# Attention beside a spectral filter on one core: the output projection as scaled fp16 parts on four column quarters, in four pieces a unit

## The chip, the cores and the metric

One Trainium2 chip; the kernel runs on one of its cores. The metric is device time in microseconds of one execution, as the median of the runs; lower is better. The parts that matter here: TensorE (PE, matrix products, with its weight loads shown as PEld), ScalarE (ACT, the exponentials), VectorE (DVE), GpSimd (POOL, which here mostly issues transfers) and SyncE (SP, which issues transfers).

## The reference

Two independent results are concatenated. A is attention with 16 query heads that share one key and one value head, over 2048 positions of 448 features (28 for each head); B is a 2-D spectral filter of a 2048 x 448 array.

```python
q = (x @ wq).reshape(B, S, H, Dh).transpose(0, 2, 1, 3)   # S=2048, H=16, Dh=28
k = x @ wk
v = x @ wv
scores = einsum("bhqd,bkd->bhqk", q, k) * Dh ** -0.5
p = softmax(scores)
o = einsum("bhqk,bkd->bhqd", p, v)
a = o.transpose(0, 2, 1, 3).reshape(B, S, H * Dh) @ wo

X = rfft2(x2)                                              # 2048 x 225
b = irfft2(X * (w_r + 1j * w_i))
return concatenate([a, b], axis=-1)
```

All inputs and outputs are float32.

## The kernel before

**Start.** The kernel projects queries, keys and values, transforms the first part of B's columns, and prepares a bound on each query's scores, so that the exponentials can run without a pass for the maxima. A planner (class `Plan`) orders this part. It is not touched.

**Main loop.** The 16 heads are four groups `g` of four; the 2048 queries are four chunks `c` of 512. The loop goes over 16 pairs (c, g), and in each over 16 blocks `kc` of 128 keys: 256 steps. A step is

- two score tiles (`scores`, line 1156): for each, eight matmuls with a stationary of 128 rows x 32 columns in fp16 and 512 moving columns, four of them side by side on the four 32-column quarters of the array. Three pairs of PSUM banks (0 to 5) take turns for them;
- two exponentials on ACT (line 1159), 128 x 1024 each, from PSUM into SBUF. Up to nine of these results may be waiting (`PAIRS`);
- one value product (`values`, line 1176): four fp32 matmuls on the four quarters, recorded as eight, into bank 6 or 7, which hold the running sum of the group.

When a group's 16 steps are over, DVE copies the sum out (`group_out`, line 1050), the denominators go through DRAM to be spread over the partitions (lines 1055 to 1063, all issued by POOL), and `group_norm` (lines 1072 to 1075) multiplies by the reciprocals and splits the result into a high part `oh` and a low part `ol`, both of type fp32r. Four spare rows of each 32-row block take copies of low parts by transfers (lines 1080 to 1085), so that fewer products are needed.

**Filler.** The bank of 6 and 7 that the current group does not use is the place for other PE work, handed out as units by queues in `work`:

- "l": what is left of B's first transform: 6 units `late_features` (line 171) and 8 units `late_points` (line 953). When the last of them has been evicted, `spectrum` starts B's long middle part on DVE, ended by a transfer through DRAM (`store`, line 901);
- "z": B's last transform, 16 units `z_unit` (line 997) and 16 units `y_unit` (line 1019), which follow that middle part;
- "w": the output projection of A, `w_unit` (line 1110): for one chunk and 128 queries, eleven fp32r matmuls of 128 x 128 by 448 columns (line 1094): high part by high weights, high by low, low by high, for four groups, where the first group lacks one of them. Twelve units for the first three chunks, available when a chunk's last group has been normalised. The fourth chunk is projected in the tail, in 48 such matmuls.

**Order.** The program order of the loop is fixed at build time by a small clock model (`clk`, `free`, `after`): it knows a nominal duration for each piece of PE, ACT and DVE work and runs the events of DVE in the order of their due times. `back` adds to `owed` at each step, `EARLY[0]` = 0.3 us until the last "l" unit is evicted, `EARLY[1]` = 0.13 until B's last transform opens, and from then on what is left divided by the steps up to step 244. A unit is placed when `owed` is positive and `filler` gives a bank (steps 1 to 13 of 16, and the bank free). `switch` adds 0.13 us to the model's PE clock whenever work on quarters and work on the whole array follow each other.

**Weights.** `wo_load` brings the seven blocks of `wo` (issued by POOL, line 756), `wo_split` makes `woh` and `wol` of them on DVE (lines 759, 761), the first four early in the loop.

**Tail.** After the loop: the last group's normalisation (lines 1247 to 1261, on ACT, DVE and POOL), beside it 36 of the 48 matmuls of the last chunk, then the last 12; ACT evicts (`last_out`, line 1105), and four transfers bring the result out.

Of the kernel before, what the change touches and what calls it, by code (L numbers as in the profile page):

```python
# [26 lines left out]
NG = 4  # L27
# [8 lines left out]
EARLY = 0.3, 0.13  # L36
# [63 lines left out]
def kernel(ctx: ExitStack, tc: tile.TileContext, t: dict):  # L100
# [623 lines left out]
    clk = {"pe": 1.9, "dve": 2.2, "act": 2.6, "mode": "s"}  # L724
# [23 lines left out]
    woh = ap.tile([128, 7, D], F32R, name="woh", bufs=1)  # L748
    wol = ap.tile([128, NG, D], F32R, name="wol", bufs=1)
# [8 lines left out]
    def wo_split(g):  # L758
        V.tensor_copy(woh[:, g], wo[g])
        if g < NG:  # L760
            TT(wol[:, g], wo[g], woh[:, g].bitcast(F32), op=ALU.subtract)
# [157 lines left out]
    work = {"l": deque(), "z": deque(), "w": deque()}  # L919
# [12 lines left out]
    def late_features(q, p):  # L932
# [10 lines left out]
        return "v", 0.86, go  # L943
# [3 lines left out]
    def late_points(q, p):  # L947
# [21 lines left out]
        return "v", 0.76, go  # L969
# [19 lines left out]
    def z_unit(q, e):  # L989
# [17 lines left out]
        return "v", 0.87, go  # L1007
# [3 lines left out]
    def y_unit(q, v):  # L1011
# [27 lines left out]
        return "v", 0.87, go  # L1039
# [7 lines left out]
    def group_out(c, g):  # L1047
        o = osb[c, g] = qraw[:, g, c * CW:c * CW + CW]
        b = acc(4 * c + g)
        V.tensor_copy(o, bank[b])  # L1050
# [15 lines left out]
    def group_norm(c, g):  # L1066
        if g == 0:
            assert c or bsl.get(5) or bsl.get(6)
            oh[c] = op.tile([128, NG, CW], F32R, name="oh")
            ol[c] = op.tile([128, NG, CW], F32R, name="ol")  # L1070
# [4 lines left out]
        TT(ol[c][:, g], o, h.bitcast(F32), op=ALU.subtract)  # L1075
        normed[c] += 1
        if c < NC - 1:
            if g == 0:
                lows[c] = dp.tile([128, CW], F32, name="lows", bufs=2)
                nc.sync.dma_start(lows[c], ol[c][:, 0].bitcast(F32))  # L1080
            rows = lows[c].rearrange("(i m r) n -> r i m n", i=4, r=4)
            if g == NG - 1:
                for r in range(4):
                    nc.sync.dma_start(oh[c][DH + r::32].bitcast(F32), rows[r, :, :4])
                    nc.sync.dma_start(ol[c][DH + r::32, 1:].bitcast(F32), rows[r, :, 4:7])
                after(clk["dve"] + 7.0, 0.0, work["w"].extend, [w_unit(c, k) for k in range(4)])

    def wo_mm(p, c, k, gs):
        s = slice(k * 128, k * 128 + 128)
        for g in gs:  # L1090
            spare = c < NC - 1
            for n, (x, w, m) in enumerate(((oh, woh, g), (oh, wol, g), (ol, woh, g + 3 * spare))):
                if n < 2 or g or not spare:
                    mm(p, x[c][:, g, s], w[:, m], start=(g == 0 and n == 0), stop=(g == NG - 1 and n == 2))  # L1094

    def wo_out(p, c, k):
        y = fp.tile([128, D], F32, name="ya", tag="al")
        V.tensor_copy(y, p)  # L1098
# [3 lines left out]
    def last_out(p, k):  # L1102
        r0 = (NC - 1) * CW + k * 128
        y = pp.tile([128, D], F32, name="yb", tag="p")
        nc.scalar.activation(y, p, AF.Copy)  # L1105
        (nc.scalar if k == 3 else nc.sync).dma_start(t["oa"][r0:r0 + 128], y)

    def w_unit(c, k):
        def go(b):
            wo_mm(bank[b][:, :D], c, k, range(NG))  # L1110
            after(clk["pe"] + 0.9, 0.65, out, b)
# [4 lines left out]
        return "s", 2.22, go  # L1116

    def switch(mode):
        if clk["mode"] != mode:
            clk["pe"] += 0.13  # L1120
            clk["mode"] = mode
# [6 lines left out]
    def filler(step):  # L1128

        b = 13 - acc(min(step, 255) // 16)  # L1130
        return b if step % 16 < 14 and step % 16 and free[b] <= clk["pe"] and any(work.values()) else None
# [256 lines left out]
```

## Time and profile before

| | |
|---|---|
| runs before | 599.91, 599.15, 600.58 us; median 599.91 |
| the profiled execution | 600.41 us, of which the profile's span is 598.3 |
| matmuls of the loop and the tail in this profile | scores x4096, values x2048, output projection x180 |
| busy, share of the span: DVE, POOL | 57%, 15% |
| DMA | 62.39 MB, mean 104 GB/s |

How to read it: a PE record's duration overlaps those of its neighbours, since matmuls are pipelined and four run side by side, so busy sums and means are larger than the time the array is held. The chain of waits gives each piece only the time up to the next piece, and its pieces can be added. A step that waits for nothing shows there as 0.86 us of scores (x16) and 0.86 us of values (x8). A stretch table gives the busy time of each engine between two points of the span, and the number of its instructions in parentheses.

### The profile page before, as it was taken

How to read it: one execution, taken by the hardware profiler on the slowest of the kernel's cores; microseconds unless marked ns; L12 is line 12 of the kernel's file. 1: busy time of each engine (PE TensorE's matmuls, PEld its weight loads, DVE VectorE, ACT ScalarE, POOL GpSimd, SP SyncE). 2: the span in 40 equal slices, each digit the busy share in tenths (PEclk: the TensorE clock that was granted, in tenths of full speed). 3: DMA queues.
4: the chain of work that ended last, by engine and by line, in shares of the span. 5: the costliest groups of instructions: out<-in, count | busy, mean ns of one | idle time of the engine just before them, and what ended most of it. 6: DMA issues, size and time to landing. Idle time of an engine off the chain costs nothing.

```text
span 598.3 us, 18675 instructions
## 1 busy us (share of the span) xinstructions
PE 589.9 (99%) x8017; PEld 297.6 (50%) x8017; DVE 338.9 (57%) x679; ACT 512.4 (86%) x580; POOL 91.2 (15%) x168
## 2 busy tenths in 40 slices
PE   9999899999999999999999999999999999999997
PEld 7877454544444444444444444454445545444446
DVE  5995715332389988889887876122443532234214
ACT  4644799999999999989898989888888886888992
POOL 1021100104210112120102012220201202020100
PEclk9999899999999999999999999999999999999999
DMA  8774712234712023331011146522333323211101
GB/s 291 245 251 121 189 50 79 64 119 128 279 60 66 19 78 105 119 94 55 27 55 41 35 163 207 152 82 71 102 104 108 128 75 131 70 41 51 38 18 61
DMA packets 37493, 62.39 MB, mean 104 GB/s; under 512 B 6405, under 2 KB 27621, under 8 KB 37401
## 3 DMA queue, kind: packets, MB, share of 16 engines
q1 hardware_dynamic: 29792, 39.99, 20.7%
q0 software_dynamic: 7472, 20.96, 11.5%
q8 instruction: 63, 1.03, 0.7%
q10 hardware_dynamic: 144, 0.23, 0.1%
q14 instruction: 22, 0.17, 0.1%
HBM read 39.94 MB, written 20.50 MB: 101 GB/s over the span
## 4 chain that ended last, share of the span: by engine, by line
PE 90%; DMA 5%; DVE 1%; ACT 1%; issue 1%; SPq 0%; POOL 0%; ACTq 0%; POOLq 0%; DVEq 0%
PE banks L1156 37%; PE banks L1176 35%; PE banks L1094 6%; PE banks L337 6%; PE banks L1019 2%; PE banks L997 2%; PE banks L171 2%; DMA t<-X 1%; DMA raw<-xw 1%; DMA sd<-qraw 1%; PE banks L953 1%; DVE X L825 1%; DMA rs<-sd 1%; DMA qa<-qd 1%; ACT yb L1105 0%
## 5 line engine op out<-in xcount | busy, mean ns | idle before, releaser
L1159 ACT ACTIVATE p<-banks 128x1024 f32<-128x1024 f32 x512 | 476.3, 1148 | 45.3 <-PE banks L1156 41.6
L1156 PE MATMUL banks<-qa,ka 128*32 128x512 f16 x4096 | 278.7, 381 | 2.2 <-DMA qa<-qd 2.2
L1176 PE MATMUL banks<-p,vs 128*32 128x512 f32 x2048 | 265.8, 592 | 0.0
L1156 PEld LDWEIGHTS <-ka 128*32 128x32 f16 x4096 | 120.9, 96 | 196.1 <-issue 149.9
L1176 PEld LDWEIGHTS banks<-p,vs 128*32 128x32 f32 x2048 | 65.6, 110 | 47.6 <-issue 1.2
L1055 POOL DMA_DIRECT2D sd<-qraw x15 | 9.2, 610 | 203.5 <-DVE qraw L1050 203.5
L1050 DVE COPY qraw<-banks 128x512 f32<-128x512 f32 x15 | 10.4, 691 | 46.6 <-PE banks L1176 46.6
L1063 POOL DMA_DIRECT2D R<-rd x60 | 30.5, 515 | 34.0 <-DMA rd<-rs 34.0
L825 DVE SCALAR_TENSOR_TENSOR X<-w,X 128x226 f32<-128x226 f32 (+2 forms) x72 | 34.0, 472 | 2.2
L1098 DVE COPY ya<-banks 128x448 f32<-128x448 f32 x12 | 7.5, 625 | 40.1 <-PE banks L1094 40.1
L1026 DVE COPY w<-banks 128x256 f32<-128x256 f32 x16 | 6.8, 425 | 41.2 <-PE banks L1019 41.2
L1003 DVE COPY z<-banks 113x512 f32<-113x512 f32 (+1 forms) x16 | 11.1, 691 | 25.7 <-PE banks L997 25.7
L1094 PE MATMUL banks<-woh,oh 128*128 128x448 f32 x64 | 24.6, 385 | 0.5 <-DVE z L1003 0.5
L337 PE MATMUL banks<-xh,wqh 128*128 128x512 f32 x64 | 24.0, 405 | 0.1
L1094 PE MATMUL banks<-wol,oh 128*128 128x448 f32 x64 | 23.2, 362 | 0.0
L337 PE MATMUL banks<-xh,wql 128*128 128x512 f32 x64 | 23.0, 390 | 0.0
L341 ACT ACTIVATE qraw<-banks 128x512 f32<-128x512 f32 x16 | 9.3, 594 | 14.9 <-PE banks L337 14.9
L1094 PE MATMUL banks<-woh,ol 128*128 128x448 f32 x52 | 18.8, 362 | 0.0
L1061 POOL DMA_DIRECT2D rd<-rs x15 | 8.2, 548 | 66.2 <-DVE rs L1060 54.8
L818 DVE SCALAR_TENSOR_TENSOR w<-X 128x113 f32<-128x113 f32 (+2 forms) x56 | 17.7, 355 | 0.1
L1094 PEld LDWEIGHTS banks<-woh,oh 128*128 128x128 f32 x64 | 12.0, 188 | 10.9 <-issue 4.2
L997 PEld LDWEIGHTS banks<-fi,c 128*32 128x32 f32 (+2 forms) x512 | 14.4, 107 | 6.1 <-issue 4.0
(127 smaller groups left out, 514.5 us busy)
## 6 DMA issues: line engine op xcount, KB each, us to landing
qa<-qd SPq DMA_DIRECT2D x64, 128.0 KB
ob<-yo SPq DMA_DIRECT2D x16, 256.0 KB
t<-bs SPq DMA_DIRECT2D x16, 226.0 KB
X<-t POOLq DMA_DIRECT2D x8, 452.0 KB, 6.5
wf<-w POOLq DMA_DIRECT2D x8, 452.0 KB, 3.7
c<-t POOLq DMA_DIRECT2D x8, 452.0 KB, 4.3
R<-rd POOLq DMA_DIRECT2D x60, 56.0 KB, 2.1
raw<-xa SPq DMA_DIRECT2D x6, 512.0 KB
```

Of the source, the lines that this page charges most:

```text
L171: mm(pa[r0:r0 + 32, e, 113 * k:113 * k + 113], f[:113, 2 * r + k, 2 * p + e, h], cs1[:113, 2 * r + k], start=True, stop=True)
L337: mm(pq[c, g], w[:, j, gs], x[:, j], start=(j == 0 and n == 0), stop=(j == 3 and n == 1))
L818: STT(out, y, sy, x, op0=ALU.mult, op1=ALU.add if c > 0 else ALU.subtract)
L825: todo(226 * n, lambda d=d, q=q: STT(both(d), t[0].rearrange("p r n f -> p r (n f)"), q, both(a), op0=ALU.mult, op1=ALU.add))
L997: mm(pz[r, j], fb["c2", q % 2][:, e, j, r], fb["fi", q % 2][:, j], start=True, stop=True)
L1003: V.tensor_copy(fb["z", q % 2, e][:w], view(bank[b], 4, 128)[:w].rearrange("p j (r n) -> p r j n", r=2))
L1019: mm(py[m:m + 32, k], cs3[:w, kind, m:m + 32], fb["z", q % 2, e][:w, r].rearrange("p j n -> p (j n)"), start=True, stop=True)
L1063: nc.gpsimd.dma_start(R[32 * i:32 * i + DH], rd[i:i + 1].to_broadcast([DH, CW]))
L1094: mm(p, x[c][:, g, s], w[:, m], start=(g == 0 and n == 0), stop=(g == NG - 1 and n == 2))
L1156: mm(bank[b + h][r], ka[:, k:k + 32], qa[c, g][:, 2 * p + h], start=True, stop=True)
L1159: nc.scalar.activation(pt[i], banks[:, b:b + 2], AF.Exp, scale=SCALE / UP / UP)
L1176: mm(bank[b][32 * i:32 * i + 32], vs[:, kc], pt[2 * st + i // 2][:, i % 2], start=(kc == 0), stop=(kc == 15))
```

## The change

Four things.

1. **Number format and shape.** `oh`, `ol`, `woh`, `wol` become fp16. The group's sums are multiplied by `scale_v` when they leave PSUM and the weights by `scale_w`, and the projected result by `back_w`. Each matmul of 128 x 128 by 448 becomes four of 128 x 32 by 448, on the four column quarters; the count of products is the same.
2. **Scales.** New function `largest`: two transfers bring four blocks of `wo`, a small one the mask; `go` takes the largest magnitudes of `vs` and of those blocks on DVE, writes them to DRAM and reads them back spread over all partitions; `fix` makes the scales of them. The weight loads move from 5.0 to 24.0 on the model's clock. The mask's load in the tail goes away.
3. **Pieces.** A `w_unit` is now one group's two or three products; it queues the next as "more", which takes precedence over all other filler, keeps the same bank, and is placed without regard to `owed` from step 13 of a group on. Other units start in steps 1 to 12.
4. **Model and pace.** `switch` goes; a piece counts 0.19 us a product; `EARLY[0]` is 0.22 in place of 0.3, and the total for the late pace counts 2.09 for a unit in place of 2.48.

The diff, without three further removals of the mode from a `return`, one further `switch("v")` and most of the unchanged lines:

```diff
@@ -33,7 +33,8 @@
-EARLY = 0.3, 0.13
+EARLY = 0.22, 0.13
+PEAK = 16384.0
@@ -721,7 +722,7 @@
-    clk = {"pe": 1.9, "dve": 2.2, "act": 2.6, "mode": "s"}
+    clk = {"pe": 1.9, "dve": 2.2, "act": 2.6}
@@ -745,8 +746,10 @@
     def wide(n):
...
-    woh = ap.tile([128, 7, D], F32R, name="woh", bufs=1)
-    wol = ap.tile([128, NG, D], F32R, name="wol", bufs=1)
+    woh = ap.tile([128, 7, D], F16, name="woh", bufs=1)
+    wol = ap.tile([128, NG, D], F16, name="wol", bufs=1)
+    scales = ap.tile([128, 5], F32, name="scales", bufs=1)
+    real, scale_v, scale_w, back_w = (scales[:, n:n + 1] for n in range(4))
@@ -756,9 +759,40 @@
     def wo_split(g):
-        V.tensor_copy(woh[:, g], wo[g])
+        V.tensor_scalar(woh[:, g], wo[g], scale_w, None, op0=ALU.mult)
...
-            TT(wol[:, g], wo[g], woh[:, g].bitcast(F32), op=ALU.subtract)
+            STT(wol[:, g], wo[g], scale_w, woh[:, g], op0=ALU.mult, op1=ALU.subtract)
+    def largest():
+        x = [scratch()[:, :2 * D].rearrange("p (g n) -> p g n", g=2) for _ in range(2)]
+        m = ap.tile([128, 4], F32, name="m", bufs=1)
+        for k in range(2):
+            nc.gpsimd.dma_start(x[k], t["wo"][:, 2 * k:2 * k + 2])
+        nc.gpsimd.dma_start(real, t["mask"])
+        def go():
+            V.tensor_reduce(m[:, 0:1], vs[:, :, :DH], axis=AX.XY, op=ALU.max, apply_absolute_value=True)
+            for k in range(2):
+                V.tensor_reduce(m[:, k + 1:k + 2], x[k], axis=AX.XY, op=ALU.max, apply_absolute_value=True)
+            TT(m[:, 1:2], m[:, 1:2], m[:, 2:3], op=ALU.max)
+            md = dp.tile([128, 2], F32, name="md")
+            nc.gpsimd.dma_start(md, m[:, :2])
+            w = scratch()[:, :256].rearrange("p (a b) -> p a b", b=2)
+            nc.gpsimd.dma_start(w, md.rearrange("(o a) b -> o a b", o=1).to_broadcast([128, 128, 2]))
+            after(clk["dve"] + 7.0, 1.0, fix, w)
+        def fix(w):
+            V.tensor_reduce(m[:, :2], w.rearrange("p a b -> p b a"), axis=AX.X, op=ALU.max)
+            V.tensor_scalar(m[:, :2], m[:, :2], 1e-30, None, op0=ALU.max)
+            V.tensor_scalar(m[:, 0:1], m[:, 0:1], 1.0 / UP, None, op0=ALU.mult)
+            V.tensor_scalar(m[:, 2:4], m[:, :2], 1.0 / PEAK, None, op0=ALU.mult)
+            TT(back_w, m[:, 2:3], m[:, 3:4], op=ALU.mult)
+            V.reciprocal(m[:, 2:4], m[:, 2:4])
+            V.tensor_copy(scale_w, m[:, 3:4])
+            V.tensor_scalar(scale_v, real, -1.0, 1.0, op0=ALU.mult, op1=ALU.add)
+            TT(real, real, m[:, 2:3], op=ALU.mult)
+            TT(scale_v, scale_v, real, op=ALU.add)
+        after(clk["dve"] + 4.0, 1.6, go)
@@ -916,7 +950,7 @@
-    work = {"l": deque(), "z": deque(), "w": deque()}
+    work = {"more": deque(), "l": deque(), "z": deque(), "w": deque()}
@@ -940,7 +974,7 @@
-        return "v", 0.86, go
+        return 0.86, go
@@ -1047,7 +1081,7 @@
     def group_out(c, g):
...
-        V.tensor_copy(o, bank[b])
+        V.tensor_scalar(o, bank[b], scale_v, None, op0=ALU.mult)
@@ -1065,24 +1099,23 @@
     def group_norm(c, g):
...
-            assert c or bsl.get(5) or bsl.get(6)
-            oh[c] = op.tile([128, NG, CW], F32R, name="oh")
-            ol[c] = op.tile([128, NG, CW], F32R, name="ol")
+            parts16 = op.tile([128, 2, NG, CW], F16, name="o16", tag=("oh", "ol")[c % 2])
+            oh[c], ol[c] = parts16[:, 0], parts16[:, 1]
...
-        TT(ol[c][:, g], o, h.bitcast(F32), op=ALU.subtract)
+        TT(ol[c][:, g], o, h, op=ALU.subtract)
...
-                lows[c] = dp.tile([128, CW], F32, name="lows", bufs=2)
-                nc.sync.dma_start(lows[c], ol[c][:, 0].bitcast(F32))
+                lows[c] = dp.tile([128, CW], F16, name="lows", bufs=2)
+                nc.sync.dma_start(lows[c], ol[c][:, 0])
...
-                    nc.sync.dma_start(oh[c][DH + r::32].bitcast(F32), rows[r, :, :4])
-                    nc.sync.dma_start(ol[c][DH + r::32, 1:].bitcast(F32), rows[r, :, 4:7])
+                    nc.sync.dma_start(oh[c][DH + r::32], rows[r, :, :4])
+                    nc.sync.dma_start(ol[c][DH + r::32, 1:], rows[r, :, 4:7])
...
     def wo_mm(p, c, k, gs):
@@ -1091,34 +1124,34 @@
             for n, (x, w, m) in enumerate(((oh, woh, g), (oh, wol, g), (ol, woh, g + 3 * spare))):
                 if n < 2 or g or not spare:
-                    mm(p, x[c][:, g, s], w[:, m], start=(g == 0 and n == 0), stop=(g == NG - 1 and n == 2))
+                    for r in range(0, 128, 32):
+                        mm(p[r:r + 32], x[c][:, g, s][:, r:r + 32], w[:, m], start=(g == 0 and n == 0),
+                           stop=(g == NG - 1 and n == 2))
...
     def wo_out(p, c, k):
...
-        V.tensor_copy(y, p)
+        V.tensor_scalar(y, p, back_w, None, op0=ALU.mult)
...
     def last_out(p, k):
...
-        nc.scalar.activation(y, p, AF.Copy)
+        nc.scalar.activation(y, p, AF.Identity, scale=back_w)
...
-    def w_unit(c, k):
+    def w_unit(c, k, g=0):
         def go(b):
-            wo_mm(bank[b][:, :D], c, k, range(NG))
-            after(clk["pe"] + 0.9, 0.65, out, b)
+            wo_mm(bank[b][:, :D], c, k, (g,))
+            if g < NG - 1:
+                work["more"].append(w_unit(c, k, g + 1))
+            else:
+                after(clk["pe"] + 0.9, 0.65, out, b)
...
         def out(b):
...
-        return "s", 2.22, go
-    def switch(mode):
-        if clk["mode"] != mode:
-            clk["pe"] += 0.13
-            clk["mode"] = mode
+        return 0.19 * (3 if g else 2), go
@@ -1128,14 +1161,16 @@
     def filler(step):
...
-        return b if step % 16 < 14 and step % 16 and free[b] <= clk["pe"] and any(work.values()) else None
+        if work["more"]:
+            return b
+        return b if step % 16 < 13 and step % 16 and free[b] <= clk["pe"] and any(work.values()) else None
...
     def fill(b):
-        kind = "l" if work["l"] else "w" if work["w"] and (last_kind[0] == "z" or not work["z"]) else "z"
-        last_kind[0] = kind
-        mode, dur, f = work[kind].popleft()
+        kind = ("more" if work["more"] else "l" if work["l"] else
+                "w" if work["w"] and (last_kind[0] == "z" or not work["z"]) else "z")
+        last_kind[0] = "w" if kind == "more" else kind
+        dur, f = work[kind].popleft()
...
-        switch(mode)
@@ -1149,7 +1184,6 @@
-        switch("v")
@@ -1182,7 +1215,7 @@
-        at = 5.0 + 6 * g if g < NG else 60.0 + 6 * g
+        at = 24.0 + 6 * g if g < NG else 60.0 + 6 * g
@@ -1196,13 +1229,13 @@
-        switch("s")
...
-        clk["pe"] += 0.605
+        clk["pe"] += 0.57
+    after(1.0, 0.0, largest)
...
-    total = 12 * 2.48 + 32 * 0.87 + 6 * 0.86 + 8 * 0.76
+    total = 12 * 2.09 + 32 * 0.87 + 6 * 0.86 + 8 * 0.76
...
     def ahead():
@@ -1224,7 +1257,7 @@
-        if spot is not None and owed > 0 or spot is not None and min(t_s, t_v) > now + 0.4:
+        if spot is not None and (owed > 0 or work["more"] and st % 16 > 12) or spot is not None and min(t_s, t_v) > now + 0.4:
@@ -1236,12 +1269,12 @@
+            while work["more"]:
+                fill(spot)
...
-    real = ap.tile([128, 1], F32, name="real", bufs=1)
-    nc.sync.dma_start(real, t["mask"])
@@ -1258,7 +1291,7 @@
-        (nc.gpsimd if k < 3 else V).tensor_tensor(l, s, h.bitcast(F32), op=ALU.subtract)
+        (nc.gpsimd if k < 3 else V).tensor_tensor(l, s, h, op=ALU.subtract)
```

More of the change, by code (lines that the diff above doesn't have):

```diff
@@ L968, in out @@
                     after(clk["dve"], 0.0, spectrum)
-        return "v", 0.76, go
+        return 0.76, go
     def spectrum():
@@ L1006, in out @@
                 after(clk["dve"] + 0.2, 0.0, work["z"].extendleft, [y_unit(q, 1), y_unit(q, 0)])
-        return "v", 0.87, go
+        return 0.87, go
     y1 = {}
@@ L1038, in last @@
             nc.sync.dma_start(t["ob"][q, h], yo)
-        return "v", 0.87, go
+        return 0.87, go
     oh, ol, osb, lows = {}, {}, {}, {}
@@ L1173, in values @@
         free[b] = inf
-        switch("v")
         for i in range(4):
```

## The prediction

> **What bounds the kernel now.** I read the page's busy shares first, then a table of three stretches of the main loop with the counts of its products in each, then the chain of waits at single steps.
>
> ```profile
> span 598.3 us, 18675 instructions
> ...
> PE 589.9 (99%) x8017; PEld 297.6 (50%) x8017; DVE 338.9 (57%) x679; ACT 512.4 (86%) x580; POOL 91.2 (15%) x168
> ```
>
> A PE that is 99% busy may still be waiting, as its records overlap. So I build its work from chain pieces, which can be added:
>
> ```profile
> 199.69 0.97 PE banks L1156 x16
> ...
> 289.27 2.41 PE banks L1094 x11
> 291.68 1.41 PE banks L1156 x24
> ...
> 408.16 0.86 PE banks L1176 x8
> 409.02 0.86 PE banks L1156 x16
> ...
> 414.18 0.87 PE banks L1019 x16
> 415.05 1.30 PE banks L1156 x24
> ```
>
> A free step is 0.86 of values (x8) + 0.86 of two score tiles (x16) = 1.72 us of PE, a score tile 0.43. Where ACT sets the pace (near 199 us) the scores take 0.97 and a step 1.83. An output unit holds PE for 2.41, and the three score tiles behind it take 1.41 where they take 1.30 behind a y unit, 3 x 0.43 and no more: 2.41 + 0.11 = 2.52 us. A y unit costs 0.87 and adds nothing behind it; z units are the same.
>
> Three stretches of the loop (columns: busy time with count of PE, PEld, DVE, ACT, POOL, then clock and DMA):
>
> ```profile
> 144.10:223.90 79.80, 79.80 (x1073) 33.64 (x1061) 61.45 (x103) 79.59 (x88) 15.05 (x28) 1.00 0.35 114
> 223.90:388.80 164.90, 164.41 (x2094) 73.05 (x2090) 125.14 (x275) 153.93 (x168) 26.36 (x48) 1.00 0.31 96
> 388.80:584.40 195.60, 195.58 (x2930) 94.56 (x2930) 64.41 (x125) 166.70 (x177) 28.65 (x52) 1.00 0.24 78
> ```
>
> The same stretches for the scores (line 1156), the values (1176) and the output products (1094) alone; the first two columns are PE and PEld:
>
> ```profile
> 144.10:223.90 79.80, 49.52 (x704) 21.70 (x700) 1.00 0.35 114
> 223.90:388.80 164.90, 92.27 (x1332) 39.06 (x1328) 1.00 0.31 96
> 388.80:584.40 195.60, 92.90 (x1408) 39.24 (x1408) 1.00 0.24 78
> ```
>
> ```profile
> 144.10:223.90 79.80, 46.98 (x360) 11.92 (x360) 1.00 0.35 114
> 223.90:388.80 164.90, 86.26 (x664) 21.21 (x664) 1.00 0.31 96
> 388.80:584.40 195.60, 92.68 (x720) 22.25 (x720) 1.00 0.24 78
> ```
>
> ```profile
> 223.90:388.80 164.90, 14.85 (x66) 11.90 (x66) 1.00 0.31 96
> 388.80:584.40 195.60, 14.87 (x66) 11.92 (x66) 1.00 0.24 78
> ```
>
> Eight score records are a tile, eight value records a step, eleven output records a unit: 88, 166.5 and 176 tiles, 45, 83 and 90 steps, and six units in each of the last two. Of 256 steps 38 are left for the stretch before 144.1. PE work against time:
>
> - second: 88 x 0.43 + 45 x 0.86 = 76.5 of 79.8: PE waits 3.3. ACT is busy for 79.59: it is the bound, PE has no filler.
> - third: 166.5 tiles and 83 steps = 143.0, six units 15.1, one z unit 0.9: 159.0 of 164.9, a wait of 5.9. ACT idles 11 us here. Both lose.
> - fourth: 176 tiles and 90 steps = 153.1, six units 15.1, the other 31 z and y units 27.0: 195.2 of 195.6. PE is the bound and waits 0.4.
>
> Why both lose in the third stretch shows at one unit:
>
> ```profile
> 292.33 5.61 ACT L1159 ACTIVATE p<-banks 128x1024 f32<-128x1024 f32 x6 [1.84 <-PE banks L1156]
> ```
>
> When a whole unit of 2.52 us stands between two score tiles, ACT runs out of filled banks and idles 1.84, and afterwards no spare PE time can be caught up, since ACT sets the pace again.
>
> **The change, part by part.**
>
> *Price of a unit.* Sixteen score matmuls, four rounds of the four quarters with 512 columns each, take 0.86: 0.215 a round, 0.42 ns a column. 448 columns make 0.188 a round, eleven rounds 2.07. The neighbours work on the same quarters, so the 0.11 behind a unit goes, as behind y units. Saved: 0.45 a unit, twelve units **5.4 us**, wherever PE sets the pace.
>
> That is the value by the nearest row, which has the same stationary shape and type. The bound above is a round that waits for its weights:
>
> ```profile
> L1156 PEld LDWEIGHTS <-ka 128*32 128x32 f16 x4096 | 120.9, 96 | 196.1 <-issue 149.9 <-DVE ka L493 2.3
> ```
>
> One load lasts 96 ns; were one of four exposed in each round, it would take 0.188 + 0.096 = 0.284. In the score rows nothing is exposed: 409.02 has 16 matmuls, hence 16 loads, in 0.86. The Trainium skill speaks against the change here ("TensorE: Matmul & The Clock Gate", Part 3: Packing small matmuls — row/col tiling): weight loads overlap running matmuls only if their row groups differ, which column quarters of 128 rows do not have, and four packed tiles were measured at 3.07 times one rather than 4. By that a round would be an estimated 0.188 x 4 / 3.07 = 0.245 us and a unit 2.69, no saving. The trace's 0.215 for 512 columns disagrees, so the sum goes by the trace.
>
> *Pieces in the third stretch.* A piece is 0.38 or 0.57 us, placed at 0.13 a step. A step then holds 1.72 + 0.13 = 1.85 us of PE against 1.83 of ACT: nearly equal. Before a piece ACT has work in stock: behind the unit above it waited 1.84 for a tile that came 2.52 + 0.43 later, so 1.1 us were in stock, more than the 0.57 of a piece. Steps 13 on flush a unit's rest at once, up to 1.7 us; a unit that starts at step 1 to 5 and is paced over about 16 steps loses one or two pieces to the flush, which I price at 0.1 a unit. Wait: 5.9 becomes 0.6. **5.3 us.** If pieces are not covered, the 5.9 stays.
>
> *Early pace.* Fourteen "l" units, each about
>
> ```profile
> 78.51 0.78 PE banks L171 x32
> ```
>
> 14 x 0.78 = 10.9: at 0.3 a step 36 steps (38, as counted above), at 0.22 some 49. The first stretch stays PE-bound (1.94 against 1.83), so stretching it costs nothing; the second shrinks from 45 steps to 34. Its wait is 0.11 a step once ACT's stock is gone (3.3 / 0.11 = 30 of 45 steps), so 19 of 34 remain: 2.1. **1.2 us.**
>
> Against this, B's middle part starts 11 steps later, and z and y units with it. The first z unit stood near step 165 (of 2094 PE records in the third stretch, 2094 - 1332 - 664 - 66 = 32 are left, one z unit, and it ends at step 38 + 45 + 83 = 166); with steps of 1.85 instead of 164.9 / 83 = 1.99 in between, I expect step 176 to 182. The chain shows the spacing at which they follow each other:
>
> ```profile
> 421.09 0.87 PE banks L997 x27
> ...
> 424.54 0.87 PE banks L997 x27
> ```
>
> 3.45 apart: 0.87 of work and 2.58 in which the bank is evicted. From step 180 on, group 11 has 9 usable steps and four groups 12 each: 57 x 1.72 = 98 us of room. 32 z and y units need 32 x 2.58 = 83, five remaining output units about a step each, 9: 92 in all. It fits, barely. Wait of the fourth stretch: 0.4 becomes 0.7, **-0.3 us**; each unit that doesn't fit costs up to 2.58 after the loop.
>
> *Scales.* POOL issues two loads of 448 KB ahead of everything else it does in the loop, and DVE waits for them in order, then for a write and a read-back.
>
> ```profile
> X<-t POOLq DMA_DIRECT2D x8, 452.0 KB, 6.5
> wf<-w POOLq DMA_DIRECT2D x8, 452.0 KB, 3.7
> c<-t POOLq DMA_DIRECT2D x8, 452.0 KB, 4.3
> R<-rd POOLq DMA_DIRECT2D x60, 56.0 KB, 2.1
> ```
>
> ```profile
> L342 DVE TENSOR_REDUCE qmx<-qraw 128x1 f32<-128x512 f32 x16 | 10.5, 679 | 0.1
> ```
>
> Loads of that size land after 3.7 to 6.5 us, two one behind the other after 4 to 8; the reductions of 448, 896 and 896 elements, at 0.68 for 512, 3 us, where the model counts 1.6; the round trip two small transfers, 4 to 5, where it allows 7. Behind DVE's waits stand the first evictions of "l" units and the split of the next group's queries, which is needed 16 steps (31 us) later. "l" units follow one another at 0.78 / 0.22 = 3.5 steps, some 7 us, which covers a slip of about 4. I put **-0.3 us**, bounds 0 and -4. Nothing here can gain, it is all added.
>
> *At no cost:* scaled evictions and splits on DVE in place of copies of the same size (DVE is busy for 57%; the third stretch, where it is fullest, has 125 of 165 and no more work than before); the weight loads moved on POOL from 5 to 24, needed first at step 83; SP's transfers of low parts with half the bytes; the mask's load that leaves SP's tail. Were DVE the bound there, each added 0.1 us in sixteen groups would be 1.6.
>
> *Tail.*
>
> ```profile
> 584.55 8.02 PE banks L1094 x39
> ```
>
> ```profile
> 592.35 0.29 DVE L1261 TENSOR_TENSOR ol<-qraw,oh 128x128 fp32r<-128x128 f32 x1
> ...
> 592.65 2.34 ACT L1105 ACTIVATE yb<-banks 128x448 f32<-128x448 f32 x4 [2.07 <-PE banks L1094]
> ```
>
> 39 of the 48 products take 8.02, 0.206 each. At 0.188 all 48 would end 0.9 earlier, but the last three wait for DVE's last low part (592.64), and ACT's four outputs, 0.59 each, become the limit: 0.5. A scale as an operand may lengthen ACT's output; the nearest row has two operands from SBUF and takes 0.815 for 512 columns, some 0.71 for 448, so 0 to 0.15 at the end:
>
> ```profile
> L527 ACT ACTIVATE qh<-qraw,cvec,mask 128x512 f16<-128x512 f32 x1 | 0.8, 815 | 1.6 <-DVE cvec L511 1.6
> ```
>
> **0.3 us** gained.
>
> Sum: 5.4 + 5.3 + 1.2 - 0.3 - 0.3 + 0.3 = **11.6 us**. The profiled execution took 600.41 us, 2.1 outside its span of 598.3; it would take 588.8. The median 599.91 lies 0.5 lower: **588.3 us**.
>
> **Rivals.**
>
> *Pieces don't hide.* Each piece costs ACT its full time, and the third stretch keeps its 5.9 us of waits. Gain 11.6 - 5.3 = 6.3: 593.6. For it: ACT and PE are within 0.02 a step of each other, so nothing is caught up quickly. Against: ACT's stock, above. 11%.
>
> *The late units don't fit* (the slower side). If z and y units start at step 190 rather than 180, 17 us of room go, 11 more than the margin of 6; that is four units over, 4 x 2.58 = 10.3, and from five units on the gain is gone. At seven over: 18.1 - 11.6 = 6.5 slower, 606.4. For it: the later start is sure. Against: DVE, which works on the middle part, idles 40 of 165 us in the third stretch now, so the middle part need not grow; and an output unit in four pieces evicts its bank once, which makes room. 6%. One to three units over is inside my range.
>
> *Weights exposed* (also slower): 0.284 a round makes a unit 3.12, twelve cost 7.2 instead of gaining 5.4, the tail loses 48 x (0.284 - 0.206) = 3.7 instead of gaining 0.3: 11.6 - 12.6 - 4.0 = 5.0 slower, 604.9. It decides from about 0.255 a round on, where 180 rounds cost 0.067 x 180 = 12. The score rows speak against it. With the estimate from the Trainium skill it would be about 598. 3%.
>
> **How the numbers follow.** Forecast 80%, the rivals 11, 6 and 3. Terms with bounds: the waits 0 to -3 more (some 3.4 of the 9.6 us of waits are left in the sum), the scales to -4, up to three units over 7.7, the unit's price within 0.01 a round (1.3): the likeliest case lies in 585.0 to 592.5. The range takes in the first rival: 585.0 to 594.5. A measurement of this kernel tells 0.2% (1.2 us) from no change. Faster 0.90 (the forecast and the first rival, less a little), same 0.02, slower 0.08.
>
> **What would show it.** Right: output products in rounds of four with 0.19 between rounds, scores behind them at their 0.43 a tile; in the middle, steps of about 1.85 with PE and ACT both full and no gap of 1.8 on ACT; the last "l" unit near step 49, the first z unit near 180, no filler between the loop's last value product and the tail. Wrong: rounds at 0.24 or more; ACT gaps of 0.4 behind single pieces; z or y units after the last step; DVE waiting for the scales so long that PE waits for an evicted bank near 75 us.

## The result, and the profile after

The changed kernel takes 589.9 us (median of 4 runs, 589.2 to 590.7) against 600.2 (599.2 to 600.6) for the kernel before on the same chip: a ratio of 0.983, with a 95% interval of 0.9815 to 0.9841. 11.6 us were forecast, 10.3 came. The profiled execution took 589.72 us with a span of 587.9, 10.7 less than before's.

The page's head and five groups of instructions (line, engine, operation, tiles, shape, count | busy us, mean ns | idle us before them and what ended it):

```profile
span 587.9 us, 19771 instructions
PE 579.7 (99%) x8557; PEld 298.5 (51%) x8557; DVE 345.9 (59%) x693; ACT 514.2 (87%) x580; POOL 94.4 (16%) x173
L1193 ACT ACTIVATE p<-banks 128x1024 f32<-128x1024 f32 x512 | 478.0, 1100 | 32.8 <-PE banks L1190 32.3
L1084 DVE TENSOR_SCALAR qraw<-banks,scales 128x512 f32<-128x512 f32 x15 | 11.3, 751 | 59.9 <-PE banks L1209 59.9
L1128 PE MATMUL banks<-woh,o 128*32 128x448 f16 x464 | 39.9, 353 | 0.0
L1128 PEld LDWEIGHTS <-o 128*32 128x32 f16 x720 | 21.7, 97 | 29.7 <-issue 22.3
L1133 DVE TENSOR_SCALAR ya<-banks,scales 128x448 f32<-128x448 f32 x12 | 8.2, 684 | 42.1 <-PE banks L1128 42.1
```

PE is still 99% busy, as before; that figure tells nothing of the 10 us. The chain of waits does. Its rows (start, us, what; scores are now line 1190, values 1209, output products 1128) first at a unit in the middle, which goes in four pieces, then at one of the few whose pieces went in one go:

```profile
225.67 0.38 PE banks L1128 x8
226.05 0.86 PE banks L1190 x16
...
229.49 0.57 PE banks L1128 x11
230.06 1.30 PE banks L1190 x24
...
242.68 0.57 PE banks L1128 x12
243.25 1.29 PE banks L1190 x24
...
471.74 2.08 PE banks L1128 x44
473.82 0.86 PE banks L1190 x16
```

44 products are eleven rounds, 2.08 / 11 = 0.189 us a round (0.188 was forecast). The three score tiles behind a piece take 1.30, the two behind the whole unit 0.86: 0.43 a tile, so nothing is added behind. A unit costs 2.08 instead of 2.52. The longest gap that ACT has behind a piece of this unit is 0.25, where a whole unit left it idle for 1.84 before:

```profile
243.79 4.69 ACT L1193 ACTIVATE p<-banks 128x1024 f32<-128x1024 f32 x5 [0.25 <-PE banks L1190]
```

The loop in four stretches, cut at the last "l" unit (step 53), the first output piece, the first z unit and the end (columns: length, then busy time with count of PE, PEld, DVE, ACT, POOL, then clock, DMA share and GB/s):

```profile
63.80:169.20 105.40, 105.38 (x1616) 51.39 (x1620) 42.12 (x87) 100.93 (x109) 15.54 (x29) 0.98 0.31 89
169.20:225.50 56.30, 56.30 (x752) 23.58 (x745) 41.09 (x58) 56.09 (x63) 12.01 (x23) 1.00 0.39 131
225.50:405.40 179.90, 179.90 (x2608) 83.64 (x2604) 145.75 (x316) 177.41 (x193) 30.92 (x55) 1.00 0.28 90
405.40:574.30 168.90, 168.90 (x2800) 86.43 (x2796) 60.91 (x118) 143.57 (x151) 25.22 (x45) 1.00 0.25 85
```

The same stretches for the scores alone, for the values alone (rows of the second and third), and for the output products alone (third and fourth):

```profile
63.80:169.20 105.40, 59.04 (x872) 27.93 (x876) 0.98 0.31 89
169.20:225.50 56.30, 35.45 (x496) 15.22 (x492) 1.00 0.39 131
225.50:405.40 179.90, 101.73 (x1536) 48.88 (x1536) 1.00 0.28 90
405.40:574.30 168.90, 79.86 (x1192) 36.25 (x1192) 1.00 0.25 85
```

```profile
169.20:225.50 56.30, 32.20 (x248) 8.22 (x248) 1.00 0.39 131
225.50:405.40 179.90, 99.14 (x764) 25.47 (x760) 1.00 0.28 90
```

```profile
225.50:405.40 179.90, 19.41 (x308) 9.17 (x304) 1.00 0.28 90
405.40:574.30 168.90, 12.64 (x220) 6.75 (x224) 1.00 0.25 85
```

Third stretch: 1536 / 8 = 192 tiles x 0.43 = 82.6, 764 / 8 = 95.5 steps x 0.86 = 82.1, 308 / 4 = 77 rounds x 0.189 = 14.5: 179.2 us of PE work in 179.9. PE waits 0.7, where the kernel before waited 5.9, and ACT, which idled 11 us there, is busy for 177.4 of 179.9. Second stretch: 62 x 0.43 + 31 x 0.86 = 53.3 of 56.3: PE waits 3.0.

### The profile page after: what moved, and what is told of

Read it like the earlier page. It is cut to its first block, busy times and chain, and to the rows that moved or that the text cites. A ratio compares the mean times of both kernels' runs of the same rounds, so it can differ in the third digit from the quotient of the medians.

```text
span 587.9 us, 19771 instructions
## 1 busy us (share of the span) xinstructions
PE 579.7 (99%) x8557; PEld 298.5 (51%) x8557; DVE 345.9 (59%) x693; ACT 514.2 (87%) x580; POOL 94.4 (16%) x173
## 4 chain that ended last, share of the span: by engine, by line
PE 97%; ACT 1%; DMA 1%; SPq 0%; issue 0%; DVE 0%; ACTq 0%
PE banks L1190 39%; PE banks L1209 37%; PE banks L338 7%; PE banks L1128 6%; PE banks L1031 2%; PE banks L1053 2%; PE banks L172 2%; PE banks L987 1%; PE banks L261 1%; DMA qa<-qd 1%; ACT yb L1140 0%; PE banks L182 0%; DMA qd<-ql 0%; ACT qh L528 0%; ACT qt L530 0%
## 5 line engine op out<-in xcount | busy, mean ns | idle before, releaser
L1190 PEld LDWEIGHTS <-ka 128*32 128x32 f16 x4096 | 128.3, 97 | 171.2 <-issue 119.9
L1209 PEld LDWEIGHTS banks<-p,vs 128*32 128x32 f32 x2048 | 68.5, 110 | 45.7 <-issue 1.8
L1084 DVE TENSOR_SCALAR qraw<-banks,scales 128x512 f32<-128x512 f32 x15 | 11.3, 751 | 59.9 <-PE banks L1209 59.9
L1128 PE MATMUL banks<-woh,o 128*32 128x448 f16 x464 | 39.9, 353 | 0.0
L1128 PEld LDWEIGHTS <-o 128*32 128x32 f16 x720 | 21.7, 97 | 29.7 <-issue 22.3
L1133 DVE TENSOR_SCALAR ya<-banks,scales 128x448 f32<-128x448 f32 x12 | 8.2, 684 | 42.1 <-PE banks L1128 42.1
L1128 PE MATMUL banks<-wol,o 128*32 128x448 f16 x256 | 24.1, 353 | 0.0
L996 DVE COPY bs<-banks 128x452 f32<-128x452 f32 x8 | 5.0, 629 | 28.0 <-PE banks L987 28.0
```

The lines of the kernel that those rows point to most:

```text
L1084: V.tensor_scalar(o, bank[b], scale_v, None, op0=ALU.mult)
L1128: mm(p[r:r + 32], x[c][:, g, s][:, r:r + 32], w[:, m], start=(g == 0 and n == 0), stop=(g == NG - 1 and n == 2))
L1190: mm(bank[b + h][r], ka[:, k:k + 32], qa[c, g][:, 2 * p + h], start=True, stop=True)
L1209: mm(bank[b][32 * i:32 * i + 32], vs[:, kc], pt[2 * st + i // 2][:, i % 2], start=(kc == 0), stop=(kc == 15))
```

## The experiments

Each edit is against the changed kernel; the ratios are to the kernel before, run beside it on the same chip. Not all runs are from one chip: the median of the kernel before lies between 599.6 and 600.8 us.

**Two edits taken apart: the parts and the pieces.** The change makes a unit cheaper and cuts it up. Three kernels give the other corners of the square.

whole_quarters: the cheap unit, uncut.

```diff
-            wo_mm(bank[b][:, :D], c, k, (g,))
-            if g < NG - 1:
-                work["more"].append(w_unit(c, k, g + 1))
-            else:
-                after(clk["pe"] + 0.9, 0.65, out, b)
+            wo_mm(bank[b][:, :D], c, k, range(NG))
+            after(clk["pe"] + 0.9, 0.65, out, b)
...
-        return 0.19 * (3 if g else 2), go
+        return 2.09, go
```

> Output units whole again (eleven products in one go), in fp16 on the quarters, all else as changed. Theory, two separate gains: the price of a unit stays at about 2.08 us, but a whole unit stands between two score tiles again. Before, such a unit of 2.52 us cost 33.1 - 17 x 1.833 = 1.94 us beyond ACT's pace; with 2.08 us it should cost 1.5, in pieces it costs 29.84 - 16 x 1.833 = 0.5. Seven units in the middle: 5 to 7 us slower than the changed kernel, 595 us (594 to 597), with gaps of about 1.4 us on ACT. Rival, format and shape alone make the gain: 590 us. Rival, pieces alone make it: 600 us.

Measured: 595.15 us (594.7 to 597.8), ratio 0.993 [0.990, 0.995]. The chain at a unit:

```profile
225.03 2.08 PE banks L1128 x44
227.11 1.29 PE banks L1187 x24
```

and ACT behind it:

```profile
227.65 7.44 ACT L1190 ACTIVATE p<-banks 128x1024 f32<-128x1024 f32 x8 [1.40 <-PE banks L1187]
```

The same 2.08, and 5.25 us more: that is what the cutting is worth, since the unit's own price has not moved. It shows as ACT's gap of 1.40 behind each whole unit of the middle: counted from the first score product, step 80 begins level with the changed kernel (155.19 us against 155.30), and step 160, with as much work done, 4.8 later (309.37 against 304.60).

pieces_full: cut in four, but each product on the whole array, as before the change.

```diff
-                    for r in range(0, 128, 32):
-                        mm(p[r:r + 32], x[c][:, g, s][:, r:r + 32], w[:, m], start=(g == 0 and n == 0),
-                           stop=(g == NG - 1 and n == 2))
+                    mm(p, x[c][:, g, s], w[:, m], start=(g == 0 and n == 0), stop=(g == NG - 1 and n == 2))
```

> Four pieces a unit and fp16 as changed, but each product on the whole array (128 x 128 by 448) in place of four quarters. Theory: the quarters matter because each piece then stands between work of the same shape. A whole-array unit of the kernel before took 2.52 us for eleven products 0.20 apart, so 0.32 for going over and back; four pieces pay that four times: 11 x 0.19 + 4 x 0.32 = 3.4 us a unit. Five late units at 1.3 more each: 6.5; seven in the middle, 16 x 1.72 + 3.4 against 29.84 for 16 steps, 1.0 each: 7. Together 603 us (600 to 606). Rival, the shape is indifferent and only fp16 and the pieces matter: 590 us.

Measured: 598.55 us (597.6 to 599.8), ratio 0.997 [0.996, 0.998]. Far above the 590 of the rival expectation, and below the other's 603. The chain:

```profile
226.07 0.49 PE banks L1127 x2
...
230.11 0.68 PE banks L1127 x3
230.79 1.41 PE banks L1188 x24
```

Three products take 0.57 (at 0.19) and 0.68 are charged; the three tiles behind take 1.41 for 1.30. Going from quarters to the whole array costs 0.11 and coming back 0.11 to 0.12, so a unit in four pieces pays 0.9 and one in one piece 0.23.

whole_full has both of these edits: the fp16 parts, their scales and the pace are left of the change.

> fp16 and scales as changed, but units whole and on the whole array, as before. Theory: fp16 by itself buys next to nothing; a unit takes 2.4 to 2.5 us (products 0.19 to 0.20 apart and 0.32 for going over and back), so neither the price nor the gaps change: 598 to 600 us. Rival, narrower weights load faster and that was the gain: 595 us or less.

Measured: 598.0 us (596.9 to 598.9), ratio 0.996 [0.995, 0.997].

```profile
226.02 2.19 PE banks L1127 x11
228.21 1.41 PE banks L1185 x24
```

2.19 + 0.12 = 2.31 a unit. So the steps are: 2.2 us for fp16 with the scales and the pace (12 units at 0.21 less are 2.5), 2.9 more for the quarters with the unit whole, 5.25 more for the pieces on quarters; the same pieces on the whole array gain nothing (0.5 slower, with intervals that overlap). The cutting is worth something only on the quarters; on the whole array, going over four times a unit, 0.9 for 0.23, takes its gain away.

halves: two pieces instead of four.

```diff
-            wo_mm(bank[b][:, :D], c, k, (g,))
-            if g < NG - 1:
-                work["more"].append(w_unit(c, k, g + 1))
+            wo_mm(bank[b][:, :D], c, k, (g, g + 1))
+            if g == 0:
+                work["more"].append(w_unit(c, k, 2))
...
-        return 0.19 * (3 if g else 2), go
+        return 0.19 * (6 if g else 5), go
```

> Each unit in two pieces of 0.95 and 1.13 us in place of four. Theory: ACT has some 1.1 us in stock at a piece, so halves are just about covered: 590 to 591.5 us, with small gaps on ACT (under 0.4) behind some of them. Rival, any piece longer than the 0.1 us a step that PE has over costs ACT its full length: 593 us or more.

Measured: 591.27 us (590.8 to 594.1), ratio 0.985 [0.983, 0.987]. ACT behind the two halves of a unit:

```profile
229.17 12.94 ACT L1193 ACTIVATE p<-banks 128x1024 f32<-128x1024 f32 x14 [0.26 <-PE banks L1190]
242.56 3.77 ACT L1193 ACTIVATE p<-banks 128x1024 f32<-128x1024 f32 x4 [0.45 <-PE banks L1190]
```

Pieces of 0.95 and 1.13 hide nearly all that pieces of 0.38 and 0.57 hide: that is about the stock of 1.1 us that the prediction read from ACT's wait.

**The scales.** const_scales leaves out the search for the largest value and weight, and with it the loads, reductions and exchange; constants stand in its place.

```diff
-            V.tensor_reduce(m[:, 0:1], vs[:, :, :DH], axis=AX.XY, op=ALU.max, apply_absolute_value=True)
...
-            nc.gpsimd.dma_start(w, md.rearrange("(o a) b -> o a b", o=1).to_broadcast([128, 128, 2]))
-            after(clk["dve"] + 7.0, 1.0, fix, w)
...
+            V.memset(m[:, 0:1], 1.0)
+            V.memset(m[:, 1:2], 0.25)
```

> The search for the largest value and weight is left out: its two loads, three reductions, the write and the read-back; the scales are made of two constants instead (1.0 and 0.25). All else as changed. Theory: the exchange is hidden, since the profile of the changed kernel shows DVE waiting 5.5 us for the read-back and PE not waiting for DVE: 589.9 us, no change within 0.6. Rival, loads and waits ahead of the loop's other work cost something after all: 586 to 589 us.

Measured: 589.61 us (588.9 to 590.0), ratio 0.981 [0.980, 0.983]: the search costs nothing that can be told here, and in the profiled execution each step of the table further down begins within 0.01 us of the changed kernel's. Its cover is thin, though. DVE in the changed kernel (start, us, engine, line, operation, tiles, count, and in brackets the idle time before it and what ended it), then POOL:

```profile
81.63 0.42 DVE L785 TENSOR_REDUCE m<-w 128x2 f32<-128x256 f32 x1 [5.54 <-DMA w<-md]
...
83.60 0.62 DVE L974 COPY spol<-banks 128x452 f32<-128x452 f32 x1
```

```profile
72.16 0.55 POOL L779 DMA_DIRECT2D md<-m  x1 [7.42 <-DVE m L777]
76.55 0.54 POOL L781 DMA_DIRECT2D w<-md  x1 [3.84 <-DMA md<-m]
```

From the store at 72.16 to the reduction at 81.63 the exchange takes 9.5 us; 4 to 5 were estimated and 7 are allowed in the order. DVE stands still for 5.54, and an "l" unit's eviction (line 974) comes late; at this pace PE reaches the unit that needs it after that.

**The early pace.** The prediction gave the pace of 0.22 instead of 0.3 a gain of 1.2 us. pace_030 undoes it.

```diff
-EARLY = 0.22, 0.13
+EARLY = 0.3, 0.13
```

> The early pace back at 0.3 us a step, all else as changed. By the recorded step of the prediction (a shorter stretch without filler gains 1.2 us): 591.1 us. Theory now: the slower pace leaves ACT without stock, and the waits of the first two stretches add up to as much at 0.22 (2.2 + 3.0) as they did before at 0.3 (1.6 + 3.3): 589.6 to 590.3 us, no change.

Measured: 596.55 us (596.1 to 597.9), ratio 0.9935 [0.992, 0.995]. Both expectations fell: the pace is worth 6.6 us. Where they come from, by the time of the first value product of a step, counted from the first score product (us, read from the traces):

```
step   before  changed  pace_030  pace_030_const  pace_030_late_z  both_z22
  16    35.00    34.55     37.03           35.55            37.05     35.77
  80   154.98   155.30    156.21          154.73           156.24    154.95
 160   310.90   304.60    304.67          303.19           304.70    303.42
 176   349.32   334.43    346.09          343.43           343.56    342.30
 192   385.58   371.44    381.81          379.15           379.28    376.82
 255   519.68   509.69    516.64          513.97           514.10    511.63
```

The early pace costs pace_030 time in two places. At step 16 it is 2.5 us behind. About 1.2 of that is one "l" unit and one score tile more that it has done by then; for the rest PE waits for the eviction that stands behind the scales on DVE. Only at step 160, where all six kernels of the table have done the same work, is it level again:

```profile
84.17 0.97 PE L987 MATMUL banks<-spol 128*32 128x226 f32 x16 [1.30 <-DVE spol L974]
```

And between steps 160 and 192 it takes 10.3 us more than the changed kernel; 3.5 of that is four z and y units that the changed kernel does later, and at step 255 it is 6.95 behind. PE there, then the stretches around it:

```profile
388.97 1.93 PE L1031 MATMUL banks<-fi,c 128*32 128x128 f32 x32 [4.32 <-DMA fi<-fi]
```

```profile
384.00:389.00 5.00, 0.68 (x12) 0.06 (x5) 0.00 (x0) 1.87 (x3) 1.99 (x4) 0.82 0.93 298
389.00:394.50 5.50, 5.50 (x65) 3.13 (x69) 0.73 (x2) 2.64 (x3) 2.03 (x4) 0.54 0.21 78
394.50:399.00 4.50, 4.50 (x76) 2.15 (x72) 1.77 (x3) 3.26 (x5) 0.00 (x0) 1.00 0.01 4
```

The first z unit stands in PE's order before its data are there. PE waits 4.32, and then the granted clock is 0.54 for 5.5 us, which is a second loss of about 2.5 (5.5 x 0.46). The Trainium skill ("TensorE: Matmul & The Clock Gate", Part 1: The HAM clock gate) has the clock halved after an idle window of about 3.4 us; this wait agrees, but not every wait of these runs does (last section).

pace_030_late_z (z placed 17.0 instead of 10.0 after its loads are issued) and pace_030_const (the constants) each take one of the two causes from pace_030.

```diff
-        after(clk["dve"] + (10.0 if q < 2 else 6.0), 0.0, work["z"].extend, [z_unit(q, 0), z_unit(q, 1)])
+        after(clk["dve"] + (17.0 if q < 2 else 6.0), 0.0, work["z"].extend, [z_unit(q, 0), z_unit(q, 1)])
```

> Early pace 0.3 as in the 596.6 us run, and the model places the first units of the last transform 7 us later (17.0 in place of 10.0 behind their load's issue), so that in the program's order the first z unit stands at step 172 in place of 168. All else as changed. Theory: at pace 0.3 the order asks for the first z unit before its data are there; PE stands idle for 4.3 us and then runs at a granted clock of 0.54 for 5.5 us, which costs another 2.5: 6.8 of the 6.6 us lost. With the later place both go: 589.5 to 591 us. Rival, the faster early pace itself costs the time (fewer steps with filler, ACT without stock): 595 us or more, whatever the place of the z unit.

> Early pace 0.3, and the search for the largest value and weight left out, with two constants for the scales. Theory: at this pace the exchange does stall PE, by some 2 us near 84 us from the start (a unit of the first transform waits for a bank behind DVE's wait for the read-back), but the stretches bound by ACT that follow take most of that back, since the run at 0.3 with the exchange is level with the changed kernel again at step 160; the stall at the first z unit stays: 595.5 to 596.5 us. Rival, the exchange is what the slower pace hides: 594 us or less.

Measured: 594.1 us (593.1 to 595.5), ratio 0.990 [0.988, 0.992], and 594.28 (593.8 to 594.7), ratio 0.990 [0.988, 0.992]. Each takes back 2.3 to 2.5 of 6.6, and neither met what was expected of it. With the constants, 1.5 us come back at step 16 and stay to step 160. With z later, z's data are there but its bank is not; PE waits 2.95 for an eviction instead, and the granted clock is 0.76 over the 5.5 us behind it.

both_z22 does both, with z placed 22.0 after its loads.

> Both remedies at once on the early pace of 0.3: the search for the largest value and weight is left out (constants 1.0 and 0.25 are used, so the scales differ from the changed kernel's), and the first z units are placed 22.0 instead of 10.0 after the group's stores, which puts the first at step 177 of the program order instead of 168. If the pace costs its 6.6 us through two waits alone, on the scales near 81 us and at the first z unit, both are gone and the kernel is level with the changed one: 589.4 to 590.4, with no wait of PE over 1 us between 380 and 400 us and the granted clock at 1.0 there. If it costs by a third thing that neither remedy touches (ACT kept short of work by the dense early units, or a bank that comes late whatever the placing), 591.5 or more.

Measured: 592.26 us (591.5 to 595.1), ratio 0.9885 [0.987, 0.990]. A third thing is left. PE, DVE and POOL there:

```profile
395.97 0.37 PE L1115 MATMUL banks<-woh,o 128*32 128x448 f16 x4 [3.08 <-DVE ya L1120]
```

```profile
393.44 0.69 DVE L1092 TENSOR_TENSOR qraw<-qraw,R 128x512 f32<-128x512 f32 x1 [11.40 <-DMA R<-rd]
...
395.23 0.68 DVE L1120 TENSOR_SCALAR ya<-banks,scales 128x448 f32<-128x448 f32 x1
```

```profile
382.25 0.74 POOL L1006 DMA_DIRECT2D c<-t  x1 [10.87 <-DMA t<-X]
...
384.78 0.54 POOL L1082 DMA_DIRECT2D rd<-rs  x1
389.76 2.03 POOL L1084 DMA_DIRECT2D R<-rd  x4 [4.44 <-DMA rd<-rs]
```

and POOL in the changed kernel:

```profile
384.63 2.02 POOL L1097 DMA_DIRECT2D R<-rd  x4 [6.05 <-DMA rd<-rs]
387.16 0.73 POOL L935 DMA_DIRECT2D t<-X  x1 [0.52 <-DVE X L859]
...
395.20 0.75 POOL L1019 DMA_DIRECT2D c<-t  x1 [6.76 <-DMA t<-X]
```

POOL issues these in the order of the program. Its load of c (an input of the z units) waits 10.87 for the store of t (the end of B's middle part), and a group's normalisation (rd, R) stands behind it; DVE waits 11.40 for R, an output unit's eviction stands behind that, and PE waits for the bank. In the changed kernel the same R was issued before the store. The pace decides which of the two comes first: with z placed at 10.0, 17.0 or 22.0, all four kernels at 0.3 have the load of c ahead of R. No run here has this order and nothing else changed.

**A slower pace still.** pace_012 puts 0.12 in place of 0.22; six z and six y units no longer fit and stand behind the loop.

> The early pace at 0.12 us a step, so slow that in the program's order 12 units of the last transform (six of each kind) stand behind the loop's last step. It tests the prediction's rival of late units that don't fit. By its price, 2.58 us a unit left over: 589.9 + 31 - 4 of waits that go = 617 us. Other theory: units behind the loop follow each other on different banks, so PE loses little, and what counts is DVE, which has 5.3 us of work on four units before it can start on the tail: 589.9 - 4 + 3 x 5.3 = 602 us (598 to 605).

Measured: 603.3 us (602.5 to 605.1), ratio 1.0054 [1.0035, 1.0073], in the range of the second expectation. 13.4 us for twelve units is 1.1 each, and part of it is two waits of PE: 3.3 at the first z unit, in the loop, and 4.3 at the y units behind the loop. room_019 (pace 0.19, and a step more in sixteen open to units other than the first output piece) and room_020_z16 (the same at 0.20, z placed at 16.0) sought a better version.

```diff
-        return b if step % 16 < 13 and step % 16 and free[b] <= clk["pe"] and any(work.values()) else None
+        return b if step % 16 < (14 if work["l"] or last_kind[0] == "w" or not work["w"] else 13) and step % 16 and free[b] <= clk["pe"] and any(work.values()) else None
```

> A version that may beat the changed kernel: early pace 0.19, and step 13 of a group open again for other units than output units, so that in the program's order nothing stands behind the loop although the last transform starts at step 188 in place of 179. Theory: the stretch without filler shrinks from 31 to 26 steps, each worth 0.1 us: 589.4 us, hardly to be told from the changed kernel. Rival, the late stretch now has waits of its own: 590.5 us or more.

> A version that may beat the changed kernel: early pace 0.20, step 13 open for other than output units, and the first units of the last transform placed at least 16.0 behind their load's issue, first z unit at step 185. Theory: nothing stands behind the loop and no data are asked for too early; 27 to 28 steps without filler in place of 31: 589.4 to 590 us. Rival, the closing transfers of the middle part meet those of a group's normalisation at this place as they did at pace 0.19: 592 us or more.

Measured: 592.62 us (592.5 to 593.4), ratio 0.987 [0.9855, 0.9885], where PE waits 3.2 for a bank at the first z unit; and 588.95 (588.2 to 590.2), ratio 0.981 [0.979, 0.983], where it waits for nothing there. The second can't be told from the changed kernel; 0.01 of pace, the placing of z and 3.7 us lie between the two.

## Why the prediction was right, and which of its steps failed

The size and both large terms held; one small term failed, and with it the reading of what the pace is for.

- *Price of a unit*, 5.4 us: 2.52 became 2.08, 12 x 0.44 = 5.3. Right, and for the reason given: the row of the scores, 0.42 ns a column, priced the new form. Of the 0.44, 0.21 came from fp16 on the whole array (2.52 against 2.31), 0.23 from no longer going over to the whole array and back (2.31 in whole_full against 2.08 in whole_quarters).
- *Pieces in the third stretch*, 5.3 us: the wait went from 5.9 to 0.7, 5.2; whole_quarters lost 5.25 by the uncut unit alone. ACT idles 2.5 us where it idled 11, and its gap behind a unit went from 1.84 to 1.40 with the cheaper unit, and to 0.25 with the pieces. Right. The first rival, that pieces don't hide, is refuted.
- *Weights exposed*: refuted by 0.189 a round. By the rule of the Trainium skill that was weighed against the trace in the prediction ("TensorE: Matmul & The Clock Gate", Part 3: Packing small matmuls — row/col tiling) it would be an estimated 0.245; the 3.07 in that estimate is the page's figure for four row tiles, not for four column quarters. The score rows decided rightly.
- *Early pace*, +1.2 us: **failed.** It was to come from fewer steps of waiting in the second stretch, 19 of 34 against 30 of 45. In the changed kernel it has 31 steps and a wait of 3.0, which at 0.11 is 27 of 31; and the first stretch, 53 steps long, waits 2.0 (105.4 us less 109 tiles x 0.43, 53 steps x 0.86 and 10.9 of "l" units) where the old one of 80.3, with 82 tiles and 38 steps, waited 1.4. Over both, 5.0 against 4.7: -0.3. Even the sign is wrong: without the exchange the pace of 0.3 is at step 160, with as much work done, 1.4 ahead of the pace of 0.22 (303.19 in pace_030_const against 304.60 in const_scales and in the changed kernel). The prediction counted the same 15 steps without a wait at both paces, as if ACT entered the stretch with the same stock; that it enters fuller at the slower pace fits the count but was not shown.
- *What the pace does instead* was not in the prediction. At 0.3 the same kernel is 6.6 us slower: the exchange of the scales then reaches PE, the first z unit comes before its data, and a group's normalisation falls behind POOL's wait for the store. In the kernel before, also at 0.3, PE has none of these three waits. The prediction treated the later start of z and y only as a loss of room. Priced at the old pace by these terms, 1.2 us less, the change would have been forecast at 589.5 us; it took 596.55, so the forecast would have been out by 7. That the kernel of the prediction had the slower pace is in this respect luck.
- *Scales*, -0.3 us: hidden, as const_scales shows, but the round trip was 9.5 us for an estimated 4 to 5; DVE stood still for 5.54, more than the 4 us of slip that the prediction took as covered, so that the cover held is luck.
- *Fourth stretch*, -0.3 us: 149 x 0.43 + 77.5 x 0.86 + 55 x 0.189 + 27.9 of z and y units make 169.0 of 168.9. It waits for nothing, +0.4. The first z unit stood at step 179 (180 forecast), the last "l" unit at 53 (49), and nothing behind the loop. The rival "the late units don't fit" did not happen, and its price of 2.58 for a unit left over was too high: 1.1 in pace_012, with two waits of PE in it.
- *Tail*, +0.3 us: 13.85 became 13.5.

The sum by the runs: 5.3 + 5.2 - 0.3 + 0.4 + 0.3 = 10.9, for 10.7 in the profiled executions.

What stays open is how much each of the three waits of the faster pace costs when alone. By the medians the constants give 2.3, the later z 2.5, both 4.3 of 6.6, and 2.4 are left. These kernels ran on three chips, so the parts are good to about 1 us: by the ratios they are 2.0, 2.1, 3.0 of 6.4, with 3.4 left, and in the profiled executions at step 255 2.7, 2.5, 5.0 of 6.95, with 1.9 left. What is left goes with a wait of 3.08 behind POOL's order, but a kernel that changes this order alone, with the store or the loads on another queue, was not tried.

## What to carry to other kernels

Filler that is put between the two halves of a loop balanced between two engines should be no larger than the work that the other engine has in stock (here about 1.1 us: ACT waited 1.84 for a tile that came 2.95 after the last), and of the same array shape as its neighbours, or each cut pays for going over twice. A pacing constant isn't priced by its own stretch: follow what it moves to the next in-order queue (DVE behind an exchange, POOL behind a store), since 0.08 of pace moved this kernel by 6.6 us. A small exchange through DRAM in the middle of a busy loop can take twice the estimate from two usual transfers (here 9.5 us for 4 to 5); look at what stands behind it in order.

## What the runs showed of the hardware

- After PE had waited 4.32 us the granted clock was 0.54 for 5.5 us, so the wait cost about half as much again (pace_030). The length of a wait alone did not decide this: 2.95 us in pace_030_late_z was followed by 0.76 over 5.5 us, while 3.08 us in both_z22 left the clock at 1.00. First pace_030_late_z, then both_z22 with its wait:

```profile
397.00:402.50 5.50, 5.50 (x80) 3.00 (x84) 2.27 (x4) 2.63 (x3) 0.00 (x0) 0.76 0.25 88
```

```profile
390.00:395.00 5.00, 2.88 (x44) 1.19 (x37) 1.49 (x3) 3.32 (x4) 1.79 (x4) 1.00 0.14 46
395.00:400.00 5.00, 4.03 (x74) 2.22 (x76) 0.91 (x2) 1.94 (x2) 0.00 (x0) 1.00 0.12 46
```

- Going over between quarters and the whole array cost 0.11 to 0.12 us each way, with two, three or eleven products between (0.49 for 0.38, 0.68 for 0.57, 2.19 for 2.08, and 1.41 for 1.29 or 1.30 in the tiles behind).
- An eviction that scales is longer than a copy: 684 and 751 ns on DVE where copies of the same shapes took 625 and 691 in the kernel before. On ACT the output took 633 ns instead of 546, but the four outputs of the tail start 0.57 us apart, before 0.60, so that the operand cost the tail nothing.
